# A gated mix of two spectral filters on one core: product rows in slot order, weights in 2052-byte rows, x in eight pieces, the gate inside the second stage

## The chip, the core and the metric

The kernel runs on one core of a Trainium2 chip. A core has a matrix engine (TensorE, "PE" in the profile, its weight loads "PEld"), a vector engine (VectorE, "DVE"), a scalar engine (ScalarE, "ACT"), GpSimd ("POOL") and a sync engine that here only issues transfers ("SP"). Each works through its own list of instructions in order, and they wait for each other by semaphores. Transfers between HBM and the on-chip memory (SBUF) run on 16 DMA engines. They are issued from two queues here, SP's and ACT's, and each queue is worked off in the order of issue. Matmuls write to PSUM, a small memory of eight banks of 128 x 512 f32, and DVE or ACT copy from there ("evict").

The metric is device time of one execution in microseconds.

## The reference

`x` is 2048 x 1024 in bf16. Two filters, A and B, each take a two-dimensional real FFT of the same `x`, multiply it by a complex weight of 2048 x 513, and transform back. A gate per row of `x` mixes the two results.

```python
def _A_ref(x, w_r, w_i):
    X = jnp.fft.rfft2(x.astype(jnp.float32), axes=(-2, -1))
    X = X * (w_r + 1j * w_i)
    return jnp.fft.irfft2(X, s=(S, D), axes=(-2, -1)).astype(jnp.bfloat16)
...
g = sigmoid((x * gate_w).sum(-1, keepdims=True))
return g * a + (1 - g) * b
```

`b` is computed from the same `x` with the weights of B.

## The kernel before

The transforms are matmuls with constant matrices. The kernel is written as a program for each engine in an order fixed by hand: every operation is added to its engine's list with the names it reads (`r=`), overwrites (`w=`) or adds to (`a=`), and waits are made from those names (L142 to L172). An engine's order is therefore the order of the lines below; nothing reorders it.

1. Loads (L252 to L266). ACT's queue carries the gate weight, copied to all 128 partitions, and a small table `SM`. SP's queue carries, alternating, four pieces of the constant `M` (256 KB each; it holds each matrix and its negative) and four pieces of `x` (1 MB each, 8 KB in each partition), then `F2`, `CK` and the weights in 32 transfers of 64 partitions by four rows of 513 elements (1026 bytes). In `R_W` a row of weights has a pitch of 514 elements, and the row index is `k1` (0 to 31) for each filter.
2. Stage 1 (L273 to L300), four chunks `c` of four rows `r`. DVE reverses half of each row (L274), then forms the gate's dot products, one row per instruction (L278, called zred below). PE makes 32 matmuls of 256 columns (L295), each pair adding the row and its reversed half, and ACT evicts four groups of 128 x 1024 (L299) into `R_F`. All of `R_F` must be there before the next stage.
3. Stages 2 and 4, a loop over 16 slots `i` (L350 to L354). Stage 2 of slot `i+1` (eight matmuls of 512 columns, L314; one eviction, L317, called CS) is placed ahead of stage 4 of slot `i` (eight matmuls, L336; two evictions, L339, called X). The CS buffers are three deep, the X buffers two deep for each of the two sets `sw` (0 and 1), and stage 2 uses PSUM banks 0 to 3 in alternating pairs, stage 4 banks 4 to 7. DVE multiplies X by the weights: four products of 128 x 1024 per slot (L348); set 0 goes to `R_A`, where `x` was, and set 1 over the weights in `R_W`. POOL copies one column of CS away (L319, called STAR).
4. Between the loops (L357 to L419). The gate: DVE spreads the dot products on diagonals (L362, 16 instructions), PE sums them over partitions (L366), ACT applies the sigmoid (L371). Column 256 is treated apart (L376 to L394), and then column 0 (L410, L412), all of it ahead of the next stage on PE.
5. Stage 5 (L436 to L461): 32 groups of 16 matmuls (L449), evicted by ACT and DVE in turn (L458), with the products of the gate and the constant `U5` among DVE's evictions (L429).
6. Stages 6 and 7 (L470 to L515): the way back to the output, 16 rounds; the constant `DI` is loaded when the last matmul of stage 5 is done, since it lies in the memory that stage 5 reads.

The operations around the change are ordered by three things: SP's queue (all loads but two), DVE's list (reversal, zreds, products and gate in that order), and the buffers just named.

Of the kernel before, what the change touches and what calls it, by code (L numbers as in the profile page):

```python
# [10 lines left out]
RW = 514  # L11
NROW = 64 * RW

# [8 lines left out]
def make_consts():  # L22

# [17 lines left out]
    M = M.reshape(128, 16, 1, 128)  # L41
    C["M"] = np.concatenate([M, -M], axis=2).reshape(128, 16 * 256)
# [49 lines left out]
    l2, k1, f = row % 2, (row // 2) % 32, row // 64  # L92
# [106 lines left out]
def bass_gated_mix__spectral_gfnet__spectral_gfnet__prompt_kernel(nc, A_x, A_w_r, A_w_i, B_x, B_w_r, B_w_i, gate_w, out):  # L199
# [10 lines left out]
    R_M = sb("R_M", 8192)  # L210
# [4 lines left out]
    STAR = sb("STAR", 16)  # L215
    XST = sb("XST", 64)
# [34 lines left out]
    GWo = 0  # L251
    dma("act", sl(RB, GWo, [(1, 1024)]), AP(gate_w.tensor, gate_w.offset, [[0, 128], [1, 1024]]), w=["gw"])  # L252
    dma("act", SM[:], cst_sm.ap(), w=["SM"])
    for c in range(4):
        dma("sp", sl(R_M, c * 1024, [(1, 1024)]).bitcast(u16), cst["M"].ap()[:, c * 1024:(c + 1) * 1024], w=[("M", c)])
        dma("sp", sl(R_A, c * 4096, [(1024, 4), (1, 1024)]), xv[:, 4 * c:4 * c + 4, :], w=[("x", c)])
    dma("sp", sl(R_M, 4096, [(1, 4096)]).bitcast(u16), cst["F2"].ap(), w=["F2"])
    dma("sp", CK[:].bitcast(u16), cst["CK"].ap(), w=["CK"])
    for c in range(4):
        for hi in range(2):  # L260
            a = 4 * c if hi == 0 else 28 - 4 * c
            for f in range(2):
                for ri in range(2):
                    src = wsrc[f, ri].rearrange("(k2 k1) l -> k2 k1 l", k1=32)[:, a:a + 4, :]
                    dst = sl(R_W, (f * 32 + a) * RW, [(RW, 4), (1, 513)], p0=64 * ri, np_=64)
                    dma("sp", dst, src, w=[("W", a // 4, f, ri)])  # L266
# [6 lines left out]
    for c in range(4):  # L273
        P.add("dve", lambda e, c=c: e.tensor_copy(  # L274
            sl(RING, (c % 3) * 2048, [(512, 4), (1, 512)]), sl(R_A, 4 * c * 1024 + 1023, [(1024, 4), (-1, 512)])),
            r=[("x", c)], w=[("xr", c % 3)])
        for r in range(4 * c, 4 * c + 4):
            P.add("dve", lambda e, r=r: e.tensor_tensor_reduce(  # L278
                out=sl(RING, 6144, [(1, 1024)]), in0=sl(R_A, r * 1024, [(1, 1024)]), in1=sl(RB, GWo, [(1, 1024)]),
                scale=1.0, scalar=0.0, op0=ALU.mult, op1=ALU.add, accum_out=ZS[:, r:r + 1]),  # L280
                r=[("x", c), "gw"], w=["zjunk"], a=["z"])

        for j in range(4):
            u = (c * 4 + j) % 4
            for q in range(4):
                r = 4 * c + q
                for h in range(2):
                    if h == 0:
                        lh = sl(R_A, r * 1024 + 128 * j, [(1, 128)])
                        rh = sl(R_M, r * 256, [(0, 2), (1, 128)])  # L290
                    else:
                        lh = sl(RING, (c % 3) * 2048 + q * 512 + 128 * j, [(1, 128)])
                        rh = sl(R_M, r * 256, [(1, 256)])
                    o = ps(u * 1024 + q * 256, [(1, 256)])
                    P.add("pe", lambda e, o=o, lh=lh, rh=rh, h=h: e.matmul(o, lh, rh, start=(h == 0), stop=(h == 1)),  # L295
                          r=[("x", c), ("M", c), ("xr", c % 3)], w=[bank(2 * u + q // 2)])
            src = ps(u * 1024, [(128, 2), (1, 128), (256, 4)])
            dst = sl(R_F, j * 4096 + 4 * c, [(2048, 2), (16, 128), (1, 4)])
            P.add("act", lambda e, s=src, d=dst: e.activation(d, s, ACT.Copy),  # L299
                  r=[bank(2 * u), bank(2 * u + 1)], a=["F1"])  # L300


    order = list(range(1, 16)) + [0]
    ALLX = ["zjunk", ("xr", 0), ("xr", 1), ("xr", 2)]

    def stage2(i):
        t = order[i]
        b0 = 2 * (i % 2)
        for cs in range(2):
            for j in range(4):  # L310
                lh = sl(R_F, (j * 2 + cs) * 2048 + t * 128, [(1, 128)])
                rh = sl(R_M, 4096 + (cs * 4 + j) * 512, [(1, 512)])
                o = ps((b0 + cs) * 512, [(1, 512)])
                P.add("pe", lambda e, o=o, lh=lh, rh=rh, j=j: e.matmul(o, lh, rh, start=(j == 0), stop=(j == 3)),  # L314
                      r=["F1", "F2"], w=[bank(b0 + cs)])
        ro = CSO + (i % 3) * 1028
        P.add("act", lambda e: e.activation(sl(RING, ro, [(513, 2), (1, 512)]), ps(b0 * 512, [(512, 2), (1, 512)]), ACT.Copy),  # L317
              r=[bank(b0), bank(b0 + 1)], w=[("CS", i % 3)] + ALLX)
        P.add("pool", lambda e: e.tensor_copy(STAR[:, t:t + 1], sl(RING, ro + 513, [(1, 1)])),  # L319
              r=[("CS", i % 3)], a=["STAR"])  # L320

    def stage4(i):
# [3 lines left out]
        k1s = (t, 32 - t) if t else (0, 16)  # L326
# [14 lines left out]
        for pm in range(2):  # L341
            k1 = k1s[pm]
            wk = [("W", k1 // 4, f, ri) for f in range(2) for ri in range(2)]
            for sw in range(2):
                xin = sl(RING, (XAO if sw == 0 else XSO) + (i % 2) * 1024 + pm * 512, [(0, 2), (1, 512)])
                win = sl(R_W, k1 * RW, [(32 * RW, 2), (1, 512)])
                dst = sl(R_A if sw == 0 else R_W, k1 * RW, [(32 * RW, 2), (1, 512)])
                P.add("dve", lambda e, d=dst, a=xin, b=win: e.tensor_tensor(out=d, in0=a, in1=b, op=ALU.mult),  # L348
                      r=[("X", sw, i % 2)] + wk, a=[("prod", sw)] + [("x", c) for c in range(4)])

    stage2(0)
    for i in range(16):
        if i + 1 < 16:
            stage2(i + 1)  # L354
        stage4(i)


    dma("sp", R_M[:].bitcast(u16), cst["U5"].ap(), w=["F2", ("M", 0), ("M", 1), ("M", 2), ("M", 3), "U5"])


    for r in range(16):
        P.add("dve", lambda e, r=r: e.tensor_scalar(out=sl(DZ, r * 128, [(1, 128)]), in0=sl(CK, IDo, [(1, 128)]),  # L362
                                                    scalar1=ZS[:, r:r + 1], scalar2=None, op0=ALU.mult),
              r=["z", "CK"], a=["DZ"])
    for q in range(4):
        P.add("pe", lambda e, q=q: e.matmul(ps(q * 512, [(1, 512)]), sl(CK, ONo, [(1, 128)]),  # L366
                                            sl(DZ, q * 512, [(1, 512)]), start=True, stop=True),
              r=["DZ", "CK"], w=[bank(q)])
    for q in range(4):
        src = ps(q * 512, [(128, 4), (1, 4), (4, 32)])  # L370
        P.add("act", lambda e, q=q, s=src: e.activation(sl(DZ, q * 512, [(1, 512)]), s, ACT.Sigmoid, scale=SM[:, 0:1]),  # L371
              r=[bank(q), "SM"], w=["DZ"] if q == 0 else [], a=["DZ"] if q else [])
# [5 lines left out]
    for sw in range(2):  # L378
        base = sw * 32
        star(ps(base + 1, [(1, 15)]), sl(CK, FB[0, 0, 1] + 64 * sw, [(1, 128)]), STAR[:, 1:16])  # L380
        star(ps(base + 17, [(1, 15)]), sl(CK, FB[0, 1, 1] + 64 * sw, [(1, 128)]), sl(STAR, 15, [(-1, 15)]))
        star(ps(base, [(1, 1)]), sl(CK, FB[1, 0, 1] + 64 * sw, [(1, 128)]), STAR[:, 0:1])
        star(ps(base + 16, [(1, 1)]), sl(CK, FB[1, 1, 1] + 64 * sw, [(1, 128)]), STAR[:, 0:1])
    P.add("dve", lambda e: e.tensor_copy(XST[:], ps(0, [(1, 64)])), r=[bank(0)], w=["XST"])
    for sw in range(2):
        P.add("dve", lambda e, sw=sw: e.tensor_tensor(
            out=sl(PST, sw * 64, [(32, 2), (1, 32)]), in0=sl(XST, sw * 32, [(0, 2), (1, 32)]),
            in1=sl(R_W, 512, [(32 * RW, 2), (RW, 32)]), op=ALU.mult),
            r=["XST"] + [("W", a, f, ri) for a in range(8) for f in range(2) for ri in range(2)], a=["PST"])
# [5 lines left out]

    for sw in range(2):
        t = R_A if sw == 0 else R_W
        T = TO[5 * sw:5 * sw + 5]
        o0 = 512 + sw * 64
        full = lambda tt: sl(tt, 0, [(RW, 64)])  # L400
        seq = [
            (ps(o0, [(1, 64)]), T[0], full(t)),
            (ps(o0, [(1, 64)]), T[0], sl(PST, sw * 64, [(1, 64)])),
            (ps(o0 + 1, [(32, 2), (1, 31)]), T[1], sl(t, 31 * RW, [(32 * RW, 2), (-RW, 31)])),
            (ps(o0 + 1, [(32, 2), (1, 31)]), T[2], sl(PST, sw * 64 + 31, [(32, 2), (-1, 31)])),
            (ps(o0, [(32, 2)]), T[3], sl(t, 0, [(32 * RW, 2)])),
            (ps(o0, [(32, 2)]), T[4], sl(PST, sw * 64, [(32, 2)])),
        ]
        for n, (o, tc, rh) in enumerate(seq):
            P.add("pe", lambda e, o=o, tc=tc, rh=rh, n=n: e.matmul(o, sl(CK, tc, [(1, 128)]), rh, start=(n == 0), stop=(n == 5)),  # L410
                  r=["CK", "PST", ("prod", sw)], w=[bank(1)])
# [166 lines left out]
```

## Time and profile before

| What | us |
|---|---|
| median of 3 runs | 181.12 (180.91 to 181.12) |
| profiled execution, its own time | 181.41 |
| its span (first to last work on the core) | 179.5 |
| PE busy | 150.9 (84%) |
| DVE busy | 120.5 (67%) |
| ACT busy | 112.9 (63%) |
| POOL busy | 11.5 (6%) |

The same span by stages, from the chain of work that ended last: stage 1 ends with its last eviction at 30.67; stages 2 and 4 on PE run from 30.72 to about 87; the work between the loops ends where stage 5 begins, at 98.50; stage 5 ends at 131.21; and the last output is done at 179.5. In stages 2 and 4 PE is busy in every slice, while in stage 1 and between the loops it idles. The profile's shares of busy time are means over stages that have different limits, so each part of the change is read in its own stage.

### The profile page before, as it was taken

What the parts mean: (1) busy time and instruction counts of PE and PEld (TensorE: products, weight loads), DVE (VectorE), ACT (ScalarE), POOL (GpSimd) and SP (SyncE); (2) the same over time, 40 slices, a digit from 0 to 9 for tenths busy, and PEclk for the clock granted to TensorE, in tenths of its full rate; (3) what the DMA queues carried; (4) which work ended last, traced back from release to release, by engine and by line L of the source; (5) the groups of instructions that cost most, each with busy time, mean ns of one, the idle gap of its engine ahead of it and who ended that gap; (6) DMA issues with size and microseconds to landing.
All of it is one profiled execution on the core that took longest, in us unless ns stands there. A gap on an engine that the chain in (4) does not pass through costs nothing.

```text
span 179.5 us, 3207 instructions
## 1 busy us (share of the span) xinstructions
PE 150.9 (84%) x1304; PEld 99.0 (55%) x1304; DVE 120.5 (67%) x233; ACT 112.9 (63%) x120; POOL 11.5 (6%) x22
## 2 busy tenths in 40 slices
PE   0099557999999999998424999999978999999991
PEld 0078445444444444443102999999966666656640
DVE  0199997067877777787974277888852787765463
ACT  2049668588898888888626355466555665565550
POOL 0000000011131131122001000000000000000000
PEclk9999999999999999999975599999999999999999
DMA  5999999999999940003800000000041213322323
GB/s 131 357 417 430 355 194 193 195 192 198 194 195 198 194 93 0 4 0 84 383 0 0 0 4 4 0 4 0 4 164 75 112 63 119 118 79 100 117 111 123
DMA packets 13038, 23.35 MB, mean 130 GB/s; under 512 B 1121, under 2 KB 9313, under 8 KB 12129
## 3 DMA queue, kind: packets, MB, share of 16 engines
q1 hardware_dynamic: 12736, 22.89, 48.4%
q10 hardware_dynamic: 288, 0.26, 0.6%
q8 instruction: 10, 0.16, 0.4%
q14 instruction: 4, 0.02, 0.1%
HBM read 18.96 MB, written 4.19 MB: 129 GB/s over the span
## 4 chain that ended last, share of the span: by engine, by line
PE 71%; DVE 13%; DMA 7%; ACT 5%; issue 2%; DVEq 0%; SPq 0%; ACTq 0%
PE PS L449 18%; PE PS L314 15%; PE PS L494 15%; PE PS L336 13%; DVE RING L278 7%; PE PS L481 6%; DMA R_A<-in_A_x_dram 4%; DMA R_A<-c_DI 3%; ACT R_F L299 2%; DVE DZ L362 1%; DVE RING L274 1%; DVE R_W L348 1%; ACT RING L339 1%; PE PS L366 1%; DVE R_A L348 1%
## 5 line engine op out<-in xcount | busy, mean ns | idle before, releaser
L339 ACT ACTIVATE RING<-PS 128x1024 bf16<-128x1024 f32 x32 | 32.8, 1024 | 3.5
L449 PE MATMUL PS<-CK,R_A 128*128 128x128 bf16 x256 | 32.6, 230 | 0.0
L449 PE MATMUL PS<-CK,R_W 128*128 128x128 bf16 x256 | 32.6, 230 | 0.0
L449 PEld LDWEIGHTS PS<-CK,R_W 128*128 128x128 bf16 x256 | 31.7, 145 | 0.0
L449 PEld LDWEIGHTS PS<-CK,R_A 128*128 128x128 bf16 x256 | 31.6, 145 | 0.0
L314 PE MATMUL PS<-R_M,R_F 128*128 128x512 bf16 x128 | 30.1, 379 | 1.2 <-ACT R_F L299 1.2
L336 PE MATMUL PS<-RING,CK 128*128 128x512 bf16 (+1 forms) x128 | 30.5, 379 | 0.6 <-ACT RING L339 0.5
L502 DVE TENSOR_TENSOR R_A<-R_A,PS 128x512 bf16<-128x512 f32 x32 | 20.6, 683 | 15.4 <-ACT R_A L498 10.2
L494 PE MATMUL PS<-R_A 128*128 128x512 bf16 x128 | 29.9, 379 | 0.5 <-DMA R_A<-c_DI 0.5
L348 DVE TENSOR_TENSOR R_A<-RING,R_W 128x1024 bf16<-128x1024 bf16 x32 | 22.0, 689 | 12.0 <-ACT RING L339 12.0
L295 PE MATMUL PS<-R_M,R_A 128*128 128x256 bf16 x64 | 16.3, 297 | 12.8 <-DVE RING L274 12.8
L485 ACT ACTIVATE R_A<-PS 128x1024 bf16<-128x1024 f32 x16 | 16.3, 1024 | 16.7 <-PE PS L481 16.7
L348 DVE TENSOR_TENSOR R_W<-RING,R_W 128x1024 bf16<-128x1024 bf16 x32 | 22.0, 689 | 6.6 <-ACT RING L339 6.6
L299 ACT ACTIVATE R_F<-PS 128x1024 bf16<-128x1024 f32 x16 | 15.2, 1032 | 12.6 <-PE PS L295 12.6
L314 PEld LDWEIGHTS PS<-R_M,R_F 128*128 128x128 bf16 x128 | 12.4, 98 | 16.4 <-ACT R_F L299 1.5
L336 PEld LDWEIGHTS PS<-RING,CK 128*128 128x128 bf16 x128 | 12.4, 98 | 16.3 <-ACT RING L339 1.6
L278 DVE CUSTOM_DVE_ANT_0 RING<-R_A,RB 128x1024 bf16<-128x1024 bf16 x16 | 19.6, 1223 | 0.4
L317 ACT ACTIVATE RING<-PS 128x1024 bf16<-128x1024 f32 x16 | 16.4, 1028 | 4.9 <-PE PS L314 4.3
L494 PEld LDWEIGHTS PS<-R_A 128*128 128x128 bf16 x128 | 11.9, 98 | 12.5 <-DMA R_A<-c_DI 0.7
L295 PE MATMUL PS<-R_M,RING 128*128 128x256 bf16 x64 | 16.2, 297 | 0.0
L319 POOL COPY STAR<-RING 128x1 bf16<-128x1 bf16 x16 | 10.6, 662 | 73.6 <-ACT RING L317 73.6
L295 PEld LDWEIGHTS PS<-R_M,R_A 128*128 128x128 bf16 x64 | 6.8, 107 | 14.6 <-DMA R_A<-in_A_x_dram 9.0
(48 smaller groups left out, 141.1 us busy)
## 6 DMA issues: line engine op xcount, KB each, us to landing
R_A<-in_A_x_dram SPq DMA_DIRECT2D x4, 1024.0 KB, 10.4
out_dram<-R_A SPq DMA_DIRECT2D x16, 256.0 KB, 2.0
R_W<-in_A_w_r_dram SPq DMA_DIRECT2D x8, 256.5 KB, 12.9
R_W<-in_A_w_i_dram SPq DMA_DIRECT2D x8, 256.5 KB, 13.0
R_W<-in_B_w_r_dram SPq DMA_DIRECT2D x8, 256.5 KB, 13.1
R_W<-in_B_w_i_dram SPq DMA_DIRECT2D x8, 256.5 KB, 13.4
R_M<-c_U SPq DMA_DIRECT2D x1, 2048.0 KB, 7.5
R_M<-c_M SPq DMA_DIRECT2D x4, 256.0 KB, 8.5
```

What stands on the lines that cost most here:

```text
L278: P.add("dve", lambda e, r=r: e.tensor_tensor_reduce(out=sl(RING, 6144, [(1, 1024)]), in0=sl(R_A, r * 1024, [(1, 1024)]), in1=sl(RB, GWo, ...
L295: P.add("pe", lambda e, o=o, lh=lh, rh=rh, h=h: e.matmul(o, lh, rh, start=(h == 0), stop=(h == 1)), r=[("x", c), ("M", c), ("xr", c % 3)], ...
L299: P.add("act", lambda e, s=src, d=dst: e.activation(d, s, ACT.Copy), r=[bank(2 * u), bank(2 * u + 1)], a=["F1"])
L314: P.add("pe", lambda e, o=o, lh=lh, rh=rh, j=j: e.matmul(o, lh, rh, start=(j == 0), stop=(j == 3)), r=["F1", "F2"], w=[bank(b0 + cs)])
L317: P.add("act", lambda e: e.activation(sl(RING, ro, [(513, 2), (1, 512)]), ps(b0 * 512, [(512, 2), (1, 512)]), ACT.Copy), r=[bank(b0), bank ...
L336: P.add("pe", lambda e, o=o, lh=lh, rh=rh, m=m: e.matmul(o, lh, rh, start=(m == 0), stop=(m == 1)), r=["CK", ("CS", i % 3)], w=[bank(b0 + ...
L339: P.add("act", lambda e, xo=xo, b0=b0: e.activation(sl(RING, xo, [(1, 1024)]), ps(b0 * 512, [(1, 1024)]), ACT.Copy), r=[bank(b0), bank(b0 ...
L348: P.add("dve", lambda e, d=dst, a=xin, b=win: e.tensor_tensor(out=d, in0=a, in1=b, op=ALU.mult), r=[("X", sw, i % 2)] + wk, a=[("prod", sw ...
L449: P.add("pe", lambda e, o=o, t=t, l0=l0, ab=ab: e.matmul(o, sl(t, l0, [(257, 128)]), sl(CK, KIAo if ab == 0 else KIBo, [(1, 128)]), start= ...
L485: P.add("act", lambda e, s=src, d=dst: e.activation(d, s, ACT.Copy), r=[bank(b0), bank(b0 + 1)], w=[("Y", r)], after=[last5])
L494: P.add("pe", lambda e, o=o, lh=lh, rh=rh, q=q: e.matmul(o, lh, rh, start=(q == 0), stop=(q == 3)), r=[("Y", r), "DI"], w=[bank(b0 + ri)])
L502: P.add("dve", lambda e, od=od, h=h: e.tensor_tensor(out=od, in0=es, in1=ps((b0 + 1) * 512, [(1, 512)]), op=ALU.add if h == 0 else ALU.sub ...
```

## The change

- Slot order: the products of slot `i` go to rows `4*i` to `4*i+3` of `R_A` and `R_W` (filter, then partner row), and the constants `U5`, the column 0 and column 256 work and `STAR` are permuted to match. One product instruction now covers 2048 elements (two filters x two rows), so there are two per slot.
- Weights are loaded in eight blocks, one for two slots, each by four transfers of 64 partitions by two rows of 2052 bytes (1026 elements; the last block goes to `R_M` by eight transfers of 3078 or 1026 bytes per partition). Block `j` lies two slots ahead of where the products of set 1 are written. A weight row starts at a pitch of 513 elements, so half of the rows start at an odd element. POOL saves the weights of column 256 (`wsave`, two copies per block) before products overwrite them.
- `M` is stored without its negatives and loaded from ACT's queue in two transfers, of 4 and 12 runs of 256 bytes per partition, followed by the gate weight and `SM` on the same queue. ACT makes the negatives (four instructions). A sigmoid on a dummy value follows ACT's transfers.
- `x` comes in eight pieces of 512 KB, alone at the head of SP's queue, at the upper end of `R_A`.
- Stage 1: of each chunk's four evictions DVE takes the last (placed after the next chunk's reversals); four zreds stay in stage 1, one per chunk, twelve move into slots 0 to 5 of the loop, two behind each slot's products. The matmuls of chunk 0 are ordered by row.
- The gate: the diagonals are made by POOL behind slot 6, and the matmuls and sigmoids stand ahead of stage 2 in slots 11 and 12, in the PSUM banks of that stage 2.
- Column 0 moves behind the third group of stage 5, with eight matmuls for each set instead of six.

```diff
-    M = M.reshape(128, 16, 1, 128)
-    C["M"] = np.concatenate([M, -M], axis=2).reshape(128, 16 * 256)
+    C["M"] = M.reshape(128, 2048)
...
+    dma("act", sl(R_M, 0, [(256, 4), (1, 128)]).bitcast(u16), cst["M"].ap()[:, 0:512], w=[("M", 0)])
+    dma("act", sl(R_M, 1024, [(256, 12), (1, 128)]).bitcast(u16), cst["M"].ap()[:, 512:2048], w=[("M", c) for c in (1, 2, 3)])
     dma("act", sl(RB, GWo, [(1, 1024)]), AP(gate_w.tensor, gate_w.offset, [[0, 128], [1, 1024]]), w=["gw"])
     dma("act", SM[:], cst_sm.ap(), w=["SM"])
-    for c in range(4):
-        dma("sp", sl(R_M, c * 1024, [(1, 1024)]).bitcast(u16), cst["M"].ap()[:, c * 1024:(c + 1) * 1024], w=[("M", c)])
-        dma("sp", sl(R_A, c * 4096, [(1024, 4), (1, 1024)]), xv[:, 4 * c:4 * c + 4, :], w=[("x", c)])
+    P.add("act", lambda e: e.activation(JNK[:, 1:2], JNK[:, 0:1], ACT.Sigmoid), r=["jnk"])
+    for c in range(8):
+        dma("sp", sl(R_A, XO + c * 2048, [(1024, 2), (1, 1024)]), xv[:, 2 * c:2 * c + 2, :], w=[("x", c)])
...
+        P.add("act", lambda e, c=c: e.activation(sl(R_M, c * 1024 + 128, [(256, 4), (1, 128)]),
+                                                 sl(R_M, c * 1024, [(256, 4), (1, 128)]), ACT.Copy, scale=-1.0),
+              r=[("M", c)], w=[("M-", c)])
...
+                if j < 7:
+                    parts = [(d0, 2052, [[(29 - 4 * j) * 513, 2], [1, 1026]], 2 * j + 1)]
+                else:
+                    parts = [(d0, 1539, [[1, 1539]], 15), (d0 + 1539, 513, [[1, 513]], 0)]
...
+    def stage1(c):
+        for q in range(0, 4, 2):
+            P.add("dve", ...)
+        if c > 0:
+            evict1(c - 1, 3, "dve")
+        zred(c)
...
+        for j in range(3):
+            evict1(c, j, "act")
...
+        for sw in range(2):
+            xin = sl(RING, (XAO if sw == 0 else XSO) + (i % 2) * 1024, [(0, 2), (512, 2), (1, 512)])
+            win = sl(wt, w0, [(2052, 2), (dpm, 2), (1, 512)])
+            dst = sl(R_A if sw == 0 else R_W, 4 * i * RW, [(2 * RW, 2), (RW, 2), (1, 512)])
...
     for i in range(16):
+        if i in (11, 12):
+            gate_rows(i - 11)
         if i + 1 < 16:
             stage2(i + 1)
+        if i % 2 == 0:
+            wsave(i // 2)
         stage4(i)
+        if i < 6:
+            zred(4 + 2 * i)
+            zred(5 + 2 * i)
+        if i == 6:
+            gate_diag()
...
+        if n == 3:
+            u = slot % 4
+            slot += 1
+            for sw in range(2):
+                column0(sw, u * 1024)
```

`gate_rows(h)` is two of the four matmuls of L366 and two of the sigmoids of L371, in banks `2h` and `2h+1`; `gate_diag` is L362 on POOL. The matmuls of column 0 for set 1 write the bank of set 0, so they wait for ACT's copy of set 0 (as before the change).

## The prediction

> **What bounds the kernel now.** I read the chain of work that ended last first, in order of time (start, duration, what).
>
> ```profile
> 8.22 0.69 DVE RING L274
> 8.92 1.13 DVE RING L278
> ...
> 25.82 1.05 PE PS L295 x8
> 26.87 0.02 issue
> 26.89 3.78 ACT R_F L299 x4
> 30.67 0.05 issue
> 30.72 3.63 PE PS L314 x16
> 34.35 1.73 PE PS L336 x8
> ...
> 90.40 2.62 DVE DZ L362 x16
> 93.02 0.05 issue
> 93.06 1.90 PE PS L366 x4
> ...
> 98.64 32.57 PE PS L449 x512
> 131.21 0.02 issue
> 131.23 4.90 DMA R_A<-c_DI
> ```
>
> Stage 1 is bound by DVE: the reversals wait behind zreds, and PE gets its last chunk at 25.82. The loop starts at 30.72 (S below) and is bound by PE, 1.73 for eight matmuls, so 3.46 per slot. From the end of the loop to 98.50 the chain is the gate and column 0. Stages 5 to 7 are PE again, and the change leaves the 48.3 us behind 131.21 alone. So it can win only before 98.50, which stands 67.8 after S.
>
> Next I read the transfers (size, us from issue to landing), since stage 1 gets new ones:
>
> ```profile
> R_A<-in_A_x_dram SPq DMA_DIRECT2D x4, 1024.0 KB, 10.4
> ...
> R_M<-c_M SPq DMA_DIRECT2D x4, 256.0 KB, 8.5
> ...
> RB<-in_gate_w_dram ACTq DMA_DIRECT2D x1, 256.0 KB, 4.9
> SM<-c_SM ACTq DMA_DIRECT2D x1, 2.0 KB, 7.2
> ```
>
> The last line is the odd one. 2 KB took 7.2 us: issued at 1.15 it landed at 8.35, just behind the first piece of x (8.20), and 2.7 after the gate weight ahead of it on ACT's queue (0.73 + 4.9 = 5.63). It has 128 rows of 16 bytes, eight for each DMA engine; the piece of x has eight rows of 8 KB. I read it so: where both queues have work an engine takes a row from each in turn, whatever the rows' length.
>
> Third, POOL beside DVE (start, us, operation, idle before):
>
> ```profile
> 35.47 0.19 POOL L319 COPY STAR<-RING 128x1 bf16<-128x1 bf16 x1 [1.53 <-ACT RING L317]
> 38.92 0.69 POOL L319 COPY STAR<-RING 128x1 bf16<-128x1 bf16 x1 [3.26 <-ACT RING L317]
> ```
>
> The same copy takes 0.19 beside an idle DVE and 0.69 when a DVE product began just before it (at 38.89): it waits out the product.
>
> **Stage 1, cost.** M now comes on ACT's queue in rows of 256 bytes: 2048 rows, 128 per engine, 32 in the first transfer; then 8 rows of the gate weight. SP's queue has 64 rows per engine for x (4 KB), 8 for F2, 8 for CK, then weights. By turns, M is complete after 128 turns and the gate weight after 136, that is with 56 weight rows per engine moved. Prices: from 15 to 16 us the engines moved 428 GB/s in long rows, so 153 ns for 4 KB, 306 for F2's 8 KB, 249 for CK's 6.5 KB. A 2052-byte row costs between 77 (at that rate) and 123 (a 1026-byte row took 16 x 1026 B / 194 GB/s = 85 ns, plus 38 for the other half): I take 100. A 256-byte row costs between 10 and 85 by the same two rows; nearer are SM's short rows, which did not slow x visibly: 20. Until 5.00 the queues moved 757 KB, worth 1.8 us at full rate, so 3.2 us are lost at the start. The sum: 3.2 + 64 x 0.173 + 8 x 0.326 + 8 x 0.269 = 19.0 for 80 turns; 48 x 0.12 = 5.8, M at 24.8; 8 x 0.177 = 1.4 and some 0.3 to land, gate weight at 26.5. Ends: 24 with the low prices, 36 with the high.
>
> The first M transfer is complete after 32 turns (8.7), its negative 0.6 later (as L498's 592 ns), so chunk 0 starts no earlier than the 9.06 of now, or some 5 later if ACT's issues are held up as SP's were (1.68 to 3.94 each from 7.33 on). That is covered, because chunk 1 waits for more: on DVE zred(0) stands ahead of chunk 1's reversals and needs the gate weight. It ends at 26.5 + 1.27 = 27.8, the reversals at 28.5. PE has idled and starts cold, as now (21 matmuls in 4.43 us, then 0.109 each): chunk 1 takes 5.7, chunks 2 and 3 3.5 each, to 41.2. ACT's three remaining negatives (26.9) and its first eviction (27.9) are covered by DVE's wait; uncovered they would cost 2.8. The last eviction, on DVE, takes 1.22 where four on ACT took 3.78. S = 42.5, that is **+11.8**. The weight blocks land from 24 on and their first use is at 48; F2 and CK are there at 19; SP's U5 waits only for the last block's readers.
>
> On this the Trainium skill speaks the other way. "DMA: Bandwidth & Descriptors", section "Queues, rings and completion order", says that an engine drains a whole packet of some 9 to 17 descriptors before it turns to the other queue. By that M would come within the first pieces of x and the first rival below would be the forecast; SM's eight rows in one turn would not have taken until 8.35, so I go by the row.
>
> **The loop, cost.** Undelayed: X of slot 15 is out at 88.35 (83.91 + 4.44), 57.6 after S, one product and a handover follow, and stage 5 starts at S + 58.9; 67.8 - 58.9 = 8.9 won from the diagonals, gate and column 0 between the loops. Against it:
> - DVE. A 1024-wide product takes 0.60 back to back, 0.53 of it elements: 2048 wide 1.13, two per slot 2.27, with two zreds (1.27) 4.80 against PE's 3.46. The first product can start at 36.56 - 30.72 = 5.8 after S, so the sixth slot's zreds end at 34.6. Two X buffers let PE run ahead, but slot 8's X needs slot 6's product (35.8), and PE's stage 4 of slot 9 starts at 36.9 where 34.6 was due. Later slots have no slack in PE: +2.6 with the second set.
> - Gate matmuls. They sit in the banks of the following stage 2, which must wait for the sigmoid. ACT's X evictions end 1.6 behind PE (82.61 against 81.00), the first sigmoid 0.65 later: 2.3 in which PE idles, twice, +4.6. CS, X and hence the products queue behind.
> - POOL. The diagonals can't start before the last zred (34.6), and STAR of slot 8 is queued behind all 16; ACT's CS of slot 11 overwrites what that STAR reads and is due at 41.3. Alone, 16 x 0.23 (spacing of the 128x64 copies) end at 38.3: no cost. If each waits out a 1.13 product as at 38.92, eight are done when DVE runs dry at 43.7, the rest take 0.3 each: STAR ends at 46.3, +5.0; at most 7.4 if DVE also waits for POOL. I take 5.0, the row being of this loop. POOL's saves of weights have two slots of slack.
>
> Sum -8.9 + 12.2 = **+3.3**, ends -1.7 (POOL free) and +5.7 (POOL at 7.4).
>
> **Stage 5, cost.** Now it begins cold (0.107 per matmul until 102.3, 1.6 us lost); PE would idle 2.4 rather than 11 us before it: -1.6. Column 0 is paid here instead: ACT evicts group 2 (1.05) before it copies set 0 (0.46), and set 1's matmuls (0.5) wait: +2.1. **+0.5**. U5, issued where stage 5 begins, lands 7.5 later, when its first user's turn comes; no cover is needed.
>
> Total +15.6 on 179.5 = 195.1 of span; the median stands 1.6 above the span (181.12 - 179.5): **196.7 us**, chance 0.47.
>
> **Rivals.**
> 1. M comes quickly and POOL gets in freely. Then 5.5 (1 MB moved by the windows), 0.6, a cold chunk 0 to 11.9, chunk 1 at the pace of ACT's evictions to 16.8, two chunks of 3.5: S = 25.1 (with 1.3 for the last eviction), -5.6; loop -1.7; +0.5: -6.8, **174.3**. For: two thirds of stage 1's DVE work is gone and M is half the bytes. Against: SM's line. Chance 0.23.
> 2. Turns go by M's rows in HBM (1 KB and 3 KB, eight each per engine), which SM's line, with one row per partition, can't exclude. Then the gate weight lands at 11 to 13, chunk 0 waits for ACT's queue and its table load (1.28) until 8.7, ACT's evictions pace chunk 1, S = 27.6: -3.1 + 3.3 + 0.5 = +0.7, **181.8**, with 177 to 184 by the loop's ends. Chance 0.22: faster 0.08, same 0.04, slower 0.10.
> 3. Products with odd rows run at one element per cycle, as L278 does (1.22 for 1024): 2.2 each, DVE bounds the loop with 16 x 4.4 + 12 x 1.27 = 85.6, some 20 more than forecast: **217**. It decides from 1.6 us per product. Chance 0.08.
>
> No line of before has an odd start with two inputs from SBUF. The skill is of two minds: "VectorE: DVE Perf Modes", "Mode 2×_1P", asks for 4-byte alignment; "Vector Engine (DVE) Microarchitecture Reference", § 5.1, says measured, it makes no difference. No run here shows it yet.
>
> **Numbers.** Range 174 to 203: from rival 1 to the forecast with S 4 later and the loop's upper end; left out are rival 3, the highest row prices and part of rival 1. The forecast's own range is 189 to 203. No change means within 0.2%, about what a measurement here tells apart. Faster: 0.23 + 0.08 = 0.31; same 0.04; slower 0.47 + 0.10 + 0.08 = 0.65.
>
> **What would show it.** Right: landing of M's second transfer over 20 us, PE idle between its 32nd and 33rd matmul, DVE's second reversal pair waiting for the gate weight; products of 1.13; POOL's diagonals near 1.1 apart and ACT waiting for POOL about slot 11; PE idle twice at the sigmoids. Wrong: S below 30, which ends the forecast whatever the loop does; or POOL done with the diagonals in 4 us.

## The result and the profile after

The changed kernel takes 205.59 us (median of four runs, 204.80 to 206.38) against 181.12 (180.91 to 181.41): slower, ratio 1.135 with a 95% interval of 1.129 to 1.141. Its profiled execution took 206.38, with a span of 204.6 against 179.5, so 25.1 us have to be found.

Two marks cut the span into three parts. The first is the start of ACT's first CS copy, some 1.95 us behind the start of the loop; the second is the first matmul of stage 5 that reads set 1 of the products.

| us | before | after | difference | forecast |
|---|---|---|---|---|
| start to first CS (stage 1) | 32.66 | 45.52 | +12.86 | +11.8 |
| first CS to stage 5 (the loop) | 65.93 | 76.49 | +10.56 | +3.3 |
| stage 5 to the issue of DI | 32.64 | 34.23 | +1.6 | +0.5 |
| the rest | 48.3 | 48.4 | +0.1 | 0 |

The transfers of stage 1 in the changed kernel (size, median us from issue to landing):

```profile
R_M<-c_M ACTq DMA_DIRECT2D x1, 384.0 KB, 23.6
RB<-in_gate_w_dram ACTq DMA_DIRECT2D x1, 256.0 KB, 25.3
...
R_M<-c_M ACTq DMA_DIRECT2D x1, 128.0 KB, 4.9
```

256 KB of gate weight took 4.9 us before and take 25.3 now. Who waits for them is in the timelines of DVE and PE in the changed kernel (start, us, engine and line, operation, idle time before it and what ended it):

```profile
27.02 1.23 DVE L300 CUSTOM_DVE_ANT_0 DZ<-R_A,RB 128x1024 bf16<-128x1024 bf16 x1 [19.40 <-DMA RB<-in_gate_w_dram]
...
28.16 0.76 DVE L309 COPY RING<-R_A 128x1024 bf16<-128x1024 bf16 x2
...
28.73 0.37 PE L327 MATMUL PS<-R_M,R_A 128*128 128x256 bf16 x1 [10.43 <-DVE RING L309]
```

The first zred stands on DVE from 7.62 to 27.02 for the gate weight. Chunk 1's reversals are queued behind it, and PE idles 10.43 for them.

In the loop, the list of PE's waits in the changed kernel names the rest (who waits, for whom, total us, times, longest):

```profile
PE PS L358 <- POOL DZ L351: 8.8, 1, 8.8
PE PS L374 <- ACT DZ L363: 4.6, 2, 3.1
```

L358 is the gate's matmul, L351 POOL's diagonals, L374 stage 2, L363 the sigmoid. The same place in the timelines of PE, ACT and POOL:

```profile
77.75 16.64 POOL L351 TENSOR_SCALAR DZ<-CK,ZS 128x128 bf16<-128x128 bf16 x16 [5.88 <-DVE ZS L300]
...
94.44 1.03 PE L358 MATMUL PS<-DZ,CK 128*128 128x512 bf16 x2 [8.85 <-POOL DZ L351]
...
94.61 1.03 ACT L377 ACTIVATE RING<-PS 128x1024 bf16<-128x1024 f32 x1 [10.15 <-POOL STAR L379]
...
98.55 3.59 PE L374 MATMUL PS<-R_M,R_F 128*128 128x512 bf16 x8 [3.07 <-ACT DZ L363]
...
106.27 1.90 PE L374 MATMUL PS<-R_M,R_F 128*128 128x512 bf16 x8 [1.54 <-ACT DZ L363]
```

POOL needs 16.64 us for sixteen diagonals. ACT was ready for CS of slot 11 at 84.46 and waited 10.15. PE waits twice more for the sigmoids, and the eight matmuls behind the first of these waits take 3.59, those behind the second 1.90: the clock had fallen while PE idled. The line of the granted clock on the changed kernel's page (40 slices of 5.1 us, tenths of full speed) shows it:

```profile
PEclk9999556999999999975599996999999999999999
```

The first dip is stage 1's wait, the second is POOL's, and the third lies at the start of stage 5.

### The profile page after: what moved, and what is told of

Read it like the earlier page. It is cut to its first block, busy times and chain, and to the rows that moved or that the text cites. A ratio compares the mean times of both kernels' runs of the same rounds, so it can differ in the third digit from the quotient of the medians.

```text
span 204.6 us, 3234 instructions
## 1 busy us (share of the span) xinstructions
PE 155.5 (76%) x1295; PEld 100.2 (49%) x1308; DVE 118.2 (58%) x192; ACT 110.2 (54%) x121; POOL 30.2 (15%) x55
## 5 line engine op out<-in xcount | busy, mean ns | idle before, releaser
L327 PE MATMUL PS<-R_M,R_A 128*128 128x256 bf16 x64 | 19.4, 334 | 22.3 <-ACT R_M L268 11.9
L374 PE MATMUL PS<-R_M,R_F 128*128 128x512 bf16 x127 | 31.6, 395 | 6.2 <-ACT DZ L363 4.6
L398 ACT ACTIVATE RING<-PS 128x1024 bf16<-128x1024 f32 x32 | 32.8, 1024 | 6.3 <-DVE R_A L409 2.8
L409 DVE TENSOR_TENSOR R_A<-RING,R_W 128x2048 bf16<-128x2048 bf16 x14 | 17.4, 1242 | 25.6 <-ACT RING L398 25.6
L300 DVE CUSTOM_DVE_ANT_0 DZ<-R_A,RB 128x1024 bf16<-128x1024 bf16 x16 | 19.5, 1221 | 19.6 <-DMA RB<-in_gate_w_dram 19.4
L566 PE MATMUL PS<-R_A 128*128 128x512 bf16 x121 | 29.2, 379 | 0.8 <-DMA R_A<-c_DI 0.5
L557 ACT ACTIVATE R_A<-PS 128x1024 bf16<-128x1024 f32 x16 | 16.3, 1024 | 16.7 <-PE PS L553 16.7
L374 PEld LDWEIGHTS PS<-R_M,R_F 128*128 128x128 bf16 x128 | 12.6, 100 | 23.0 <-ACT DZ L363 6.0
L327 PEld LDWEIGHTS PS<-R_M,R_A 128*128 128x128 bf16 x64 | 7.6, 119 | 24.8 <-issue 22.6
L327 PE MATMUL PS<-R_M,RING 128*128 128x256 bf16 x64 | 19.3, 333 | 0.0
L379 POOL COPY STAR<-RING 128x1 bf16<-128x1 bf16 x16 | 6.3, 398 | 81.6 <-ACT RING L377 81.6
L351 POOL TENSOR_SCALAR DZ<-CK,ZS 128x128 bf16<-128x128 bf16 x16 | 16.6, 1059 | 5.9 <-DVE ZS L300 5.9
L409 DVE TENSOR_TENSOR R_W<-RING,R_W 128x2048 bf16<-128x2048 bf16 x14 | 17.1, 1219 | 0.0
```

The costliest lines, as they stand in the source:

```text
L300: P.add("dve", lambda e: e.tensor_tensor_reduce(out=sl(DZ, 0, [(1, 1024)]), in0=sl(R_A, XO + r * 1024, [(1, 1024)]), in1=sl(RB, GWo, [(1, ...
L351: P.add("pool", lambda e, r=r: e.tensor_scalar(out=sl(DZ, r * 128, [(1, 128)]), in0=sl(CK, IDo, [(1, 128)]), scalar1=ZS[:, r:r + 1], scala ...
L398: P.add("act", lambda e, xo=xo, b0=b0: e.activation(sl(RING, xo, [(1, 1024)]), ps(b0 * 512, [(1, 1024)]), ACT.Copy), r=[bank(b0), bank(b0 ...
L566: P.add("pe", lambda e, o=o, lh=lh, rh=rh, q=q: e.matmul(o, lh, rh, start=(q == 0), stop=(q == 3)), r=[("Y", r), "DI"], w=[bank(b0 + ri)])
```

## The experiments

"First CS", "loop" and "stage 5" are the three parts of the table above, each from that run's own profile. The loop is the part to compare where stage 1 is left alone: kernels with the changed kernel's own stage 1 have their first CS anywhere from 43.62 to 45.81.

| kernel | first CS | loop | stage 5 | span |
|---|---|---|---|---|
| before | 32.66 | 65.93 | 32.64 | 179.5 |
| after | 45.52 | 76.49 | 34.23 | 204.6 |
| M on SP's queue | 30.73 | 76.32 | 34.52 | 189.8 |
| M in long rows | 27.94 | 76.68 | 33.03 | 186.1 |
| gate weight first | 51.49 | 76.34 | 34.52 | 210.9 |
| diagonals on DVE | 45.64 | 66.10 | 33.02 | 193.2 |
| diagonals as copies | 43.77 | 71.55 | 34.19 | 198.0 |
| diagonals with a constant | 43.62 | 73.29 | 34.51 | 200.0 |
| diagonals spread | 43.95 | 68.66 | 34.52 | 195.7 |
| STAR on DVE | 45.58 | 75.58 | 33.03 | 202.6 |
| DVE's diagonals, gate in free banks | 45.81 | 62.99 | 34.49 | 191.8 |
| DVE's diagonals, one zred per slot | 45.14 | 63.59 | 34.42 | 191.6 |
| all of it, column 0 in one bank | 26.17 | 58.84 | 33.00 | 166.5 |
| all of it, column 0 in two banks | 26.67 | 58.80 | 32.48 | 166.6 |

### Stage 1: whose rows, and in which queue

**M on SP's queue, ahead of x.**

```diff
-    dma("act", sl(R_M, 0, [(256, 4), (1, 128)]) ...
-    dma("act", sl(R_M, 1024, [(256, 12), (1, 128)]) ...
+    dma("sp", sl(R_M, 0, [(256, 4), (1, 128)]) ...
+    dma("sp", sl(R_M, 1024, [(256, 12), (1, 128)]) ...
```

> M's two transfers, in the same 256-byte rows, go out on SP's queue ahead of x, so that only the gate weight and SM are left on ACT's. Theory (rows of two queues are moved in turn, so that M on ACT's queue gets one 256-byte row for each long row of x, F2, CK and the weights): without another queue's long rows between its own, M's 128 rows per engine are done within 3 to 9 us, the gate weight lands by 8 rather than 27.0, zred(0) does not hold the reversals of chunk 1, and the loop starts near 28 to 31 us rather than 43.5; span 189 to 193. Rival (256-byte rows take about 0.18 us each by themselves, whatever stands beside them): M's second transfer still lands near 24, x comes only behind it, and the loop starts at 50 or later; span over 210.

**M in long rows, still on ACT's queue.**

```diff
+    M = M.reshape(128, 16, 1, 128)
+    C["M"] = np.concatenate([M, -M], axis=2).reshape(128, 16 * 256)
...
+    dma("act", sl(R_M, 0, [(1, 1024)]) ...
+    dma("act", sl(R_M, 1024, [(1, 3072)]) ...
```

> M comes with its negatives, twice the bytes, in rows of 2 KB and 6 KB, 16 per engine rather than 128, still on ACT's queue beside x; the four negations on ACT are left out. Theory (turns go row by row): M's 16 rows per engine are through after 16 rows of x, by 8 to 12 us, the gate weight by 14; stage 1 is then held by x and DVE alone and the loop starts at 26 to 31; span 187 to 192. Rival (the second queue is starved by SP's whatever its rows): M's second transfer lands later than 20 us and the loop starts at 40 or later; span over 200.

**Gate weight and SM ahead of M on ACT's queue.**

```diff
+    dma("act", sl(RB, GWo, [(1, 1024)]), AP(gate_w.tensor, ...
+    dma("act", SM[:], cst_sm.ap(), w=["SM"])
     dma("act", sl(R_M, 0, [(256, 4), (1, 128)]) ...
     dma("act", sl(R_M, 1024, [(256, 12), (1, 128)]) ...
```

> The gate weight and SM are issued ahead of M on ACT's queue; M keeps its 256-byte rows there. It tells which of the two late transfers holds chunk 1. Theory (by turns M needs 128 turns wherever the gate weight stands): the gate weight lands by 8, zred(0) and the reversals of chunk 1 no longer wait, but the second M transfer still lands at 25 to 27, chunk 1 starts on it and its negation near 27 to 29, and the loop starts at 41 to 44; span 202 to 206. Rival (the gate weight's wait on DVE is the only hold, M would be early): chunk 1 starts before 20 and the loop before 34; span under 196.

The transfers of the three kernels, in the order above (size, us from issue to landing):

```profile
R_M<-c_M SPq DMA_DIRECT2D x1, 384.0 KB, 6.7
RB<-in_gate_w_dram ACTq DMA_DIRECT2D x1, 256.0 KB, 5.2
```

```profile
R_M<-c_M ACTq DMA_DIRECT2D x1, 768.0 KB, 9.1
...
RB<-in_gate_w_dram ACTq DMA_DIRECT2D x1, 256.0 KB, 10.6
```

```profile
R_M<-c_M ACTq DMA_DIRECT2D x1, 384.0 KB, 30.3
RB<-in_gate_w_dram ACTq DMA_DIRECT2D x1, 256.0 KB, 6.4
```

The same 384 KB in the same 256-byte rows took 6.7 us on x's own queue and 23.6 beside it; twice the bytes in long rows took 9.1 beside it. So neither the short row nor the second queue is slow by itself. The second M transfer has 96 rows per engine. On SP's queue they arrived between 6.16 and 7.93, 0.018 us each; on ACT's between 5.6 and 24.80, 0.20 each. That is the time of one long row of the other queue between two of M's, as the turns by row have it. The turns can also be counted. From 8 to 16 us of the changed kernel SP's queue (q1) and ACT's (q10) moved so many packets (rows, and on SP's queue some 90 small ones beside them; then MB and share of time):

```profile
q1 hardware_dynamic: 776, 3.01, 95.1%
q10 hardware_dynamic: 775, 0.20, 11.5%
```

One packet of ACT's queue went for each of SP's, though a row of x is sixteen times as long as one of M. The rivals of the first two runs are out, and the spans are as expected (189.8) or 1 us better (186.1).

The third run has a miss. The gate weight came at 7.1, as expected, but M at 32.4, not at 25 to 27, and the kernel is slower than the changed one. The 96 rows took 0.19 each here too. But in the changed kernel M's first 32 rows were in by 5.6, about when x's first piece was (4.81): from 4 to 5 us ACT's queue moved 392 packets and SP's only 45, so that M went through a gap in x's stream. Here the gate weight and SM were ahead, and the first M transfer came at 14.38. What the expectation left out is this head start; why x's queue moved so little in that stretch is open. Chunk 1 starts 2.9 behind M, at 35.27: ACT's negatives and evictions, which DVE's wait covers in the changed kernel, now stand in front of it, the 2.8 that the prediction had put on them uncovered.

### The diagonals

**On DVE.** With `r` from 0 to 15:

```diff
-            P.add("pool", lambda e, r=r: e.tensor_scalar(out=sl(DZ, r * 128, ...
+            P.add("dve", lambda e, r=r: e.tensor_scalar(out=sl(DZ, r * 128, ...
```

> The sixteen gate diagonals are made by DVE, behind the products of slot 6, rather than by POOL; nothing else changes. Theory (STAR of slot 8 stands behind sixteen POOL operations of 0.6 us and more, and ACT's CS of slot 11 waits for it): ACT's wait of 10.15 us at slot 11 goes, DVE's sixteen cost at most 16 x 0.2 = 3.2 us, part of it hidden; span 194 to 199, and the gates' own stalls in PE remain. Rival (ACT's wait only takes the place of one for DVE's products, which run at the same pace): the span falls by under 3, to 202 or more.

The loop is 10.4 shorter, the span 11.4, slightly more than expected: PE's clock no longer dips there, and stage 5 has no dip either (33.02). DVE makes the sixteen in 2.69 us.

**STAR on DVE**, the diagonals left on POOL. It tests whom the diagonals hold up.

```diff
-        P.add("pool", lambda e: e.tensor_copy(STAR[:, i:i + 1], ...
+        P.add("dve", lambda e: e.tensor_copy(STAR[:, i:i + 1], ...
```

> Only the sixteen one-column copies to STAR move, from POOL to DVE; POOL keeps the diagonals as they are. Theory (as the prediction put it: ACT's CS of slot 11 waits for STAR of slot 8, which is queued behind the diagonals): without that queue ACT's wait of 10.15 us goes and the span falls by 8 to 10, to 195 to 197. Rival (the first gate matmul stands at the same place in PE's program and reads the diagonals itself, so that the wait only changes its name): PE still idles 8 to 9 us before the gate matmuls, CS of slot 11 is gained at most 1 to 2 us, span 202 to 205.

The rival is right: 0.9 us of the loop. The PE, DVE and ACT timelines of this kernel:

```profile
95.58 1.03 PE L358 MATMUL PS<-DZ,CK 128*128 128x512 bf16 x2 [9.57 <-POOL DZ L351]
...
95.88 1.24 DVE L409 TENSOR_TENSOR R_W<-RING,R_W 128x2048 bf16<-128x2048 bf16 x1 [7.21 <-POOL WST L421]
...
96.65 1.27 ACT L363 ACTIVATE DZ<-PS,SM 128x512 bf16<-128x512 f32 x2 [8.41 <-PE PS L358]
```

ACT's wait for STAR is gone, and PE's gate matmul, in the same slot, waits for the diagonals itself. A third waiter shows too: DVE's product overwrites weights that POOL has yet to save (WST), and the saving is queued behind the diagonals. The prediction had given it two slots of slack, which 17 us of diagonals use up. So three waits for one cause stood side by side.

**As plain copies**, and **with a constant**, which price the operation. Both leave the gate's sums out.

```diff
-            P.add("pool", lambda e, r=r: e.tensor_scalar(out=..., in0=sl(CK, IDo, [(1, 128)]),
-                                                        scalar1=ZS[:, r:r + 1], scalar2=None, op0=ALU.mult),
+            P.add("pool", lambda e, r=r: e.tensor_copy(sl(DZ, r * 128, [(1, 128)]), sl(CK, IDo, [(1, 128)])),
```

```diff
-                                                        scalar1=ZS[:, r:r + 1], scalar2=None, op0=ALU.mult),
+                                                        scalar1=0.5, scalar2=None, op0=ALU.mult),
```

> POOL's sixteen diagonals become plain copies of the same 128x128 identity, so the gate's sums are left out of them; place, count and bytes are the same. It prices the operation. Theory (0.60 us alone is the price of multiplying by one number per partition; a copy of this width costs what the 128x64 copy suggests, 0.23 to 0.46): the last nine, beside an idle DVE, take 2.1 to 4.1 us rather than 5.24, ACT waits 8 to 9 us at slot 11. Rival (POOL pays per element, 128 of them 0.55 to 0.6, whatever the operation): the last nine take 5 us or more and ACT's wait stays at 10, span within 0.5 of 204.6.

> The sixteen diagonals stay TENSOR_SCALAR on POOL, but multiply by the constant 0.5 rather than by one number per partition that is read from ZS, so the gate's sums are left out of them. In the changed kernel four of them took 2.39 to 2.57 us each beside DVE's products (two products' time) and the other twelve 0.60; a plain copy took 1.23 to 1.29 (one product) and 0.285. Theory (the second wait and the second 0.3 us belong to reading the per-partition number): with a constant each takes 1.2 to 1.3 beside a product and 0.28 to 0.35 alone, sixteen in 11 to 12.5 us, span near 198. Rival (they belong to the multiplication, whatever its operand): 2.4 and 0.6 stay, sixteen in 16 to 17 us, span 202 to 205.

POOL's timeline taken at two moments in each kernel, first beside a product of DVE, then beside an idle DVE (start, us, operation): the changed kernel, the copies, the constant.

```profile
80.30 2.39 POOL L351 TENSOR_SCALAR DZ<-CK,ZS 128x128 bf16<-128x128 bf16 x1
...
88.56 0.60 POOL L351 TENSOR_SCALAR DZ<-CK,ZS 128x128 bf16<-128x128 bf16 x1
```

```profile
79.60 1.28 POOL L351 COPY DZ<-CK 128x128 bf16<-128x128 bf16 x1
...
86.44 0.28 POOL L351 COPY DZ<-CK 128x128 bf16<-128x128 bf16 x1
```

```profile
84.63 1.26 POOL L351 TENSOR_SCALAR DZ<-CK 128x128 bf16<-128x128 bf16 x1
...
86.36 0.53 POOL L351 TENSOR_SCALAR DZ<-CK 128x128 bf16<-128x128 bf16 x1
```

DVE's products follow one another every 1.14 us, and up to 1.23 apart beside POOL's work. A copy, or a multiplication by a constant, takes one such step; a multiplication by a number read per partition takes two (2.39 to 2.57). That one waits for the other for a whole instruction agrees with the Trainium skill, "SBUF — State Buffer", "SBUF: two separate sides": of a DVE operation with two inputs from SBUF and a GpSimd operation that reads SBUF, the one that starts first holds a shared port pair for the whole of its instruction, and the other is blocked. It says nothing of a second wait. The second wait belongs to the reading of the number, as the theory of the last run had it. The price alone does not: 0.53 with the constant against 0.60 with the read number and 0.28 for the copy, so most of the difference to a copy is the multiplication, and there its rival is right. With the constant the sixteen took 14.0 us and the span was 200.0, between the two expectations. The copies' price alone was at the theory's low end, but ACT's wait fell to 5.06 rather than 8 to 9, which the expectation had missed: each copy waited out one product rather than two.

**Spread over the slots**, each diagonal behind its own sum. The sums' unused product goes to a free half of `RB`.

```diff
-        if i == 6:
-            gate_diag()
+        if i < 7:
+            gate_diag(range(4) if i == 0 else (2 + 2 * i, 3 + 2 * i))
```

> POOL still makes the sixteen diagonals, but each behind its own sum, two per slot from slot 1 on (four behind slot 0), rather than all sixteen behind the last sum; the sums' unused product goes to a free half of RB, so that it does not overwrite them. Theory (the cost is the bunch of sixteen in front of STAR of slot 8, not POOL's work as such): at 1.5 us each two per slot take 3 of a slot's 4.7 us, STAR is late by no more than 3, ACT's wait at slot 11 goes, and so does the cold clock behind it; span 190 to 195, a little below the version with the diagonals on DVE (193.2), since DVE is spared 2.7. Rival (POOL beside DVE slows DVE, or STAR is late in every slot): products grow over 1.2 us, or ACT waits for STAR in slots 3 to 8; span 198 or more.

The loop fell by 7.8, less than with DVE's diagonals. All but two of the diagonals now stand beside a busy DVE for at least part of their time, and sixteen take 29.8 us in all rather than 16.6. POOL falls behind, as its row and ACT's show:

```profile
61.24 5.02 POOL L351 TENSOR_SCALAR DZ<-CK,ZS 128x128 bf16<-128x128 bf16 x2
...
79.20 1.03 ACT L377 ACTIVATE RING<-PS 128x1024 bf16<-128x1024 f32 x1 [3.80 <-POOL STAR L379]
```

Two need 4 to 5 us of a slot's 4.69, with STAR and the saved weights queued behind them, and ACT still waits for STAR, 5.8 us over three slots. So the bunch was only part of it: beside a busy DVE this operation was dear wherever it stood. The span, 195.7, lies between the two expectations.

### The gate's banks and DVE's load

Both on top of the version with DVE's diagonals (loop 66.10).

**The gate in free banks.**

```diff
-        if i in (11, 12):
-            gate_rows(i - 11)
         if i + 1 < 16:
             stage2(i + 1)
+        if i in (12, 13):
+            gate_rows(i - 12)
```

> On top of the version with the diagonals on DVE (span 193.2): the gate's matmuls come behind the following stage 2, in the pair of banks that CS has just emptied, and their sigmoid stands on ACT between CS and X. Theory (PE's idle 2.52 and 1.81 ahead of the two stage 2 is the sigmoid queued behind X in the banks that stage 2 needs): both go, ACT's four sigmoids (2.5 us in all) lie beside PE's work for a good part; span 189 to 191. Rival (ACT is as full as PE at that point, so the sigmoids' 2.5 us come back as a wait of stage 4 or 2): span 192 to 193.

**One zred per slot**, three ahead of the first product.

```diff
+    for r in (4, 5, 6):
+        zred(r)
     for i in range(16):
...
-        if i < 6:
-            zred(4 + 2 * i)
-            zred(5 + 2 * i)
-        if i == 6:
+        if i < 9:
+            zred(7 + i)
+        if i == 9:
             gate_diag()
```

> On top of the version with the diagonals on DVE (span 193.2): three sums go ahead of the first product, into DVE's 5.9 us of idle time at the start of the loop, and the other nine one per slot over slots 0 to 8 rather than two per slot over slots 0 to 5. Theory (two sums make DVE's slot 4.69 against PE's 3.46, which puts the first gate matmul 3.6 us behind S + 39.8): DVE's slot becomes 3.45, PE never waits for X before the gates; span 189 to 191. Rival (the gates' own stalls take up DVE's arrears anyway): PE reaches the gates earlier but stage 5 starts within 1 us of where it did; span 192 or more.

The gate's own edit gained 3.1 in the loop. Before it PE idled 2.52 and 1.81 there; after it, by PE's timeline, it idles 0.17 and 0.28 (first two lines: with DVE's diagonals alone; the others: with the gate in free banks):

```profile
90.12 1.90 PE L374 MATMUL PS<-R_M,R_F 128*128 128x512 bf16 x8 [2.52 <-ACT DZ L363]
...
95.99 1.90 PE L374 MATMUL PS<-R_M,R_F 128*128 128x512 bf16 x8 [1.81 <-ACT DZ L363]
```

```profile
94.86 1.90 PE L374 MATMUL PS<-R_M,R_F 128*128 128x512 bf16 x8 [0.17 <-ACT DZ L363]
...
99.21 1.90 PE L374 MATMUL PS<-R_M,R_F 128*128 128x512 bf16 x8 [0.28 <-ACT DZ L363]
...
104.12 2.17 PE L395 MATMUL PS<-RING,CK 128*128 128x512 bf16 x8 [1.24 <-ACT RING L398]
```

0.7 of it comes back as ACT's arrears at the last slot (1.24, against 0.53 without the edit). One zred per slot gained 2.5: PE no longer waits for X before the gate, but the diagonals, now behind slot 9, come 2.65 late for its matmul in slot 11, so the rival holds in part:

```profile
85.77 0.61 PE L358 MATMUL PS<-DZ,CK 128*128 128x512 bf16 x2 [2.65 <-DVE DZ L351]
```

Both spans, 191.8 and 191.6, stand just above the 189 to 191 expected, because stage 5 had a clock dip in both (34.49 and 34.42, against 33.02 without).

### All together

M goes out contiguous, in rows of 1 KB and 3 KB per partition, and its negatives are made into a block of their own; the diagonals, the zreds and the gate are placed as in the three runs above. The second of the two versions also gives each set of column 0 its own bank.

```diff
+    dma("act", sl(R_M, 0, [(1, 512)]) ...
+    dma("act", sl(R_M, 512, [(1, 1536)]) ...
...
-                    rh = sl(R_M, r * 256, [(1, 256)])
+                    rh = sl(R_M, r * 128, [(2048, 2), (1, 128)])
...
-        o0 = base + sw * 64
+        o0 = base + sw * 512
```

> All that the runs so far point to, on the changed kernel: M in one row of 1 KB and one of 3 KB per partition on ACT's queue, its negatives made on ACT into a block of their own; the diagonals on DVE behind slot 9; three sums ahead of the first product and one per slot after; the gate's matmuls behind the following stage 2 at slots 12 and 13. Theory (the losses add): the loop starts at 24 to 26, first CS to stage 5 takes 60 to 61 us, stages 5 to 7 82 to 83; span 167 to 171, time 169 to 173, a ratio of 0.93 to 0.955 to the kernel before. Rival (one loss covers another, above all DVE, which has now 53 us of work in a loop of 57): PE waits for products or diagonals in slots 10 to 14 and the span stays above 174.

> The same, with column 0's two sets in two PSUM banks rather than one, so that the second set's matmuls need not wait for ACT's copy of the first. Theory (the prediction's 2.1 us of column 0 are mostly ACT's wait and that copy): PE's wait of 1.05 us between the two sets goes, span 0.9 to 1.2 under that of the version with one bank. Rival (group 2's eviction ahead of it on ACT holds PE's next group anyway): no difference over 0.3.

169.21 us (168.21 to 171.34, four runs) and 168.95 (168.73 to 169.22) against 181.54 for the kernel before in the same series: ratios 0.931 (0.926 to 0.937) and 0.932 (0.928 to 0.936). Both beat both kernels. The span, 166.5, and the loop, 58.8, are a little better than the theory had them. PE's timeline and the clock line of the first version:

```profile
69.16 0.59 PE L357 MATMUL PS<-DZ,CK 128*128 128x512 bf16 x2
...
73.05 0.59 PE L357 MATMUL PS<-DZ,CK 128*128 128x512 bf16 x2
...
80.33 2.17 PE L394 MATMUL PS<-RING,CK 128*128 128x512 bf16 x8 [1.24 <-ACT RING L397]
```

```profile
PEclk9999999999999999999999999999999999999999
```

Neither gate matmul waits, and the clock line has no dip left (it doesn't show the start: the first 14 matmuls of chunk 0 still stand up to 0.21 apart, the later ones 0.11). The second bank can't be told from one by the times: spans of 166.6 and 166.5, as the rival has it. PE's wait between the two sets is gone, but that execution had a clock dip in stage 5. Its stage 5 took 32.48, against 34.2 to 34.5 in the other executions with a dip and 33.0 without. That would be a gain of 1.7 to 2.0 if the dips were alike; it is more than the wait of 1.1 that went, so they are not quite, and the gain is not shown.

## Why the prediction was wrong, and where right

Faster or slower was right, and so was the order of the causes. The forecast of 196.7 was 9 short and 205.6 lies above the range. Of the span's 9.5 us of miss, 1.1 lie in stage 1, 7.3 in the loop and 1.1 in stage 5. In the forecast's own terms the loop's 7.3 are POOL (ACT waited 10.15 rather than 5.0) and the clock (2.1 that were not in the sum), with the other terms as forecast. This split inside the loop is book-keeping, since the losses overlap: PE itself idled 8.85 for the diagonals. What an experiment shows is the two together: with the diagonals on DVE, POOL's wait and the cold clock went and the loop was 10.4 shorter, net of the 2.69 that DVE then spent on them.

**Stage 1, +11.8: right, +12.9.** Turns by row, M's second transfer beyond 20 us, the zred behind the gate weight, chunk 1 behind the zred: each is in the rows above, and the first two runs undo them. That M landed at 24.8, as forecast to the tenth, is luck in part: two errors cancelled. The first M transfer landed at 5.6, not 8.7, in the gap of x's stream, so that only one of the six weight transfers in the sum had landed by then (at 24.14); but x, F2 and CK took until 22.71 rather than 19.0. ACT's issues were held up 6.67 us, and chunk 0 started at 11.91; chunk 1 waited for more, so that this was covered as said. "DMA: Bandwidth & Descriptors" of the Trainium skill, "Queues, rings and completion order", with whole packets of 9 to 17 descriptors before a turn, is not what these runs show: 0.20 us for each 256-byte row beside the other queue, 0.018 without it, and 775 packets of one queue for 776 of the other are a turn for each row.

**The loop without the gate, -8.9: right within 1.8.** The prediction's undelayed loop would be 65.93 - 8.9 = 57.0; with the losses removed it is 58.8, with the gate's own matmuls in it.

**DVE's zreds, +2.6: right in size.** With DVE's diagonals PE's waits for X before the gate are 0.43, 0.81 and 0.98, 2.2 in all. The run that spreads the zreds gained 2.5, but not by these waits alone: PE waited 2.65 for the diagonals in their place, and the first sigmoid held it 0.78 rather than 2.52. In the changed kernel itself only two of the waits stand (0.42 and 0.79); the third is lost in POOL's.

**The gate's banks, +4.6: right as a wait,** 3.07 and 1.54 in the changed kernel; only 3.1 of 4.3 could be won back.

**POOL, +5.0: the step that failed; ACT waited 10.15 for STAR.** The sentence was: "If each waits out a 1.13 product as at 38.92, eight are done when DVE runs dry at 43.7, the rest take 0.3 each". DVE ran dry at 43.5 after S, as forecast. But the row at 38.92 is a copy, and so are the rows behind 0.23 to 0.3. A multiplication by a number per partition took the time of two products (2.39, where the signs of being right had 1.1), so four were done rather than eight. Alone it takes 0.60, so that the end of the fourth and the other twelve kept POOL busy for 7.35 us beyond that moment, where eight at 0.3 were to take 2.4. That is the 5 us. The bounds had the same flaw: all of them were made from copies, so 7.4 was no upper end. That POOL waits out DVE and holds up STAR was right; the size was taken from another operation. And the named waiter was one of three: with STAR off POOL's queue only 0.9 was won.

**The clock, not in the sum inside the loop.** The forecast had a cold start in stage 1, but put nothing on the clock behind POOL's wait. In PE's 8.85 us of idle time it fell to half, so that the gate's first two matmuls took 1.03 rather than 0.59 and the eight behind them 3.59 rather than 1.90: 2.1.

**Stage 5, +0.5: right where the clock holds** (33.0 against 32.64, in four runs), 1.1 short in this execution, whose clock dipped just behind its start. The forecast had taken that off as "-1.6, no longer cold".

**The rivals.** Rival 1's early M is what the two repairs give (first CS 27.94 and 30.73, that is S of 26.0 and 28.8, for 25.1), but POOL does not get in freely. Rival 2's turns by rows in HBM are out: M's rows are 1 KB and 3 KB there, and it came at 24.8. Rival 3 is out: products of 2048, half of whose weight rows start at an odd element, follow each other every 1.14 us, no slower per element than the old ones of 1024 at 0.60. That is as the Trainium skill's "Vector Engine (DVE) Microarchitecture Reference", § 5.1, has it and against the 4-byte alignment that "VectorE: DVE Perf Modes", "Mode 2×_1P", asks for.

## What to carry to other kernels

A second queue was no free lane here: beside a queue with long rows a transfer cost its number of rows times the other queue's row time. So count rows per engine and give the second queue long rows, or issue it ahead on the same queue. Price an operation by a row of the same operation with the same kinds of operands on the same engine; where there is none, the bound has to be wide. And before work is placed on an engine that looks idle, list everything that waits for its result in the slot where it is due; taking away one waiter shows little if another reads the same thing.

## What the runs showed of the hardware

- POOL beside DVE's 1.14 us products: copy 1.23 to 1.29, multiplication by a constant 1.26 (the first 1.45), by a number per partition 2.39 to 2.57; beside an idle DVE 0.28, 0.53 and 0.60. DVE makes the last kind in 2.69 / 16 = 0.17.
- PE's granted clock fell to half in or just behind waits of 3.2 us and more (the 3.2 with the diagonals spread) and held in waits of up to 2.65 (one zred per slot). "TensorE: Matmul & The Clock Gate" of the Trainium skill, "HAM oscillation — how this bites in real kernels", puts the limit at about 3.4 us: near, though the wait of 3.2 is under it and the dips of the next point don't fit.
- At the start of stage 5 the clock dipped (in the changed kernel to 0.5 for 3 us) in nine of the thirteen profiles after the first, though PE had waited no longer than 1.24 in the 10 us before; in the other four, with the same waits, it did not. Stage 5 took 1.2 to 1.5 us longer with it, in the kernels with one bank for column 0. What sets it off is open.
